# Moving softmax exponentials, a gate row and the last residual inside a TensorE-bound transformer block

## The chip, the cores and the metric

The kernel runs on one core of one Trainium2 chip. The metric is the device time of one launch in microseconds (us). Three plain runs of the kernel before took 769.52, 769.94 and 769.98 us; their median is 769.94 us. A separate execution was recorded by the profiler and took 769.86 us.

## The reference

The block has 2048 tokens of width D = 640. One conditioning vector `c` gives six rows of modulation. Attention is linear attention with a learned feature map (32 heads of 20 features), and the feed-forward part squares its ReLU. Everything is fp32.

```python
mod = (silu(c) @ w_mod).reshape(1, 6, 1, 640)
sa, ca, ga, sb, cb, gb = mod[:, 0], ..., mod[:, 5]
h = layernorm(x) * (1 + ca) + sa
q, k, v = heads(h @ wqkv)
pq = q @ w_phi;  pk = k @ w_phi                 # per head, 20 x 20
phi_q = concat(softmax(pq), softmax(-pq));  phi_k likewise
o = phi_q (phi_k^T v) / (phi_q (phi_k^T 1) + 1e-6)
x = x + ga * (o @ wo)
h = layernorm(x) * (1 + cb) + sb
r = relu(h @ w1 + b1) ** 2                      # 640 -> 1728
x = x + gb * (r @ w2 + b2)
```

## The kernel before

Tokens are worked on in 16 tiles of 128, mostly as 8 pairs (`NB` = 8, index `j`). A product of two fp32 matrices is made of three matmuls on a high and a low part of each operand; the high part is a ScalarE copy that rounds, and the low part a VectorE subtraction (`lo`, line 88). The program has three stages.

**Projections.** For every tile, k, v and (for tiles 0 to 11) q are projected, and phi_k^T v and its row sums are accumulated. The exponentials of q for tiles 0 to 11 (`KEPT` = 12) are computed here and parked in DRAM. The products of `c` with the sixth part of `w_mod`, which give the gate `gb`, are summed by VectorE in `gb_mac`, and TensorE turns them (`mod_turn`) into `mt5`, of which `mod_sum(5, gate_b)` makes a [128, 5] column tile. A gate is needed as a row that is the same on all 128 partitions: `spread_row` writes the columns element by element to a DRAM tile `GD` and reads that tile back with a broadcast. `biases` loads `b2` as such a row, before into a tile `b2s`.

**Attention output.** From about 255 to 389 us the loop over `j` runs with the order of TensorE, VectorE, ScalarE and GpSimd written out by hand. Per tile, `e_prod`, `e_recip` and `e_scale` (VectorE, and small steps on GpSimd) form the denominators and scale the q features. Per pair, `tr_e(j, gs)` turns the scaled features on TensorE in six groups (`te` in the profile) and ScalarE copies each group out (`ept`); `num` multiplies by phi_k^T v; `num_hi` (ScalarE) and `num_lo` (VectorE) split the result into `ot`; `do_wo` multiplies by `wo` (`pwo`). In iteration `j`, TensorE works on the output product of pair `j` and on `tr_e` and `num` of pair `j + 1`. The six `ept` copies of a pair share five buffers (tag `s4`), so the sixth copy waits until `num` has read the first. Tiles 12 to 15 still lack their exponentials: `q_chain(t, False)` makes the differences (`spread`, VectorE, tile `eq`), `exps` applies two exponentials of 128x640 on ScalarE, and `q_sums` reduces them on VectorE. `SPREAD` and `SUMS` say at which `j` tiles 13 and 14 get these steps. Each `do_wo` ends in ScalarE copies (`at`); `p_hi`, `p_lo` and `p_load` split and load the feed-forward weights in between.

**Feed-forward.** The loop over `j` (pairs) and `n` (7 pairs of feature blocks) runs `up` (matmul, ScalarE ReLU with bias, VectorE square), `split_a` and the `down` of the step before. From `PLAIN` = 2 on, most `down` steps use a Strassen-like scheme of seven products, with accumulators in PSUM banks `acc` (named "1" to "7" and "x"). "3" and "x" are the two halves of one bank, `acc3x`; "6" and "7" share the bank with tag `p67`. The results of a pair are combined (`first_combos`, `end`), multiplied by the gate row `gb_b` (`by_gate`) and added to the residual `XR`, to which the gated bias `bb` was added before (`add_bias`). For the last pair the final three blocks are plain products, which `last_downs` ends: quarter by quarter ("3", "x", "2", "4") it does the last products, and VectorE reads each finished quarter with `by_gate`, adds it to `Y` and stores it.

Of the kernel before, what the change touches and what calls it, by code (L numbers as in the profile page):

```python
# [8 lines left out]
F32 = mybir.dt.float32  # L9
# [42 lines left out]
def kernel(  # L52
# [64 lines left out]
    def row(tag, name):  # L117
        return (pc if tag in ("s3", "s4") else mem).tile([P, D], F32, tag=tag, name=name, bufs=BUFS[tag])
# [384 lines left out]
            nc.gpsimd.dma_start(w[2 * n : m, 0], w[2 * n : m, 1])  # L503

    ga_b = row("s4", "ga_b")
    b2s = []

    def biases():
        b2s.append(row("s1", "b2s"))
        nc.sync.dma_start(b2s[0], bass.AP(tensor=b2.tensor, offset=b2.offset, ap=[[0, P], [1, D]]))  # L510

    GB = []

# [19 lines left out]
    }  # L533
    gate_a = const.tile([P, NC], F32, name="gate_a")
    gate_b = const.tile([P, NC], F32, name="gate_b")
    LAST_COL = {7: (2, gate_a), 9: (3, cols_b[:, 0:5]), 11: (4, cols_b[:, 5:10])}
    SIDE = {
        2: lambda: mod_mac(2, 0, 1, 2),
# [590 lines left out]
    e_scale(3)  # L1129
    load_e(6)  # L1130
    e_prod(4)
    SPREAD, SUMS = {1: 1, 3: 2}, {2: 1, 4: 2}
    ln0 = None
    for j in range(NB):
        nxt = j + 1 < NB
        b, c = 2 * j + 5, 2 * j + 6
        te_at = (0, 1) if 0 < j < 6 else (1, 2)
        if j == 4:
            load_x1(0)
        if j < 5:  # L1140
            p_load()
        if j != 5:
            e_prod(b)
        e_recip(b - 1)
        e_scale(b - 1)
        if j == 5:
            q_chain(KEPT + 3, False)
            add_x(0, 0, 1)
            nc.vector.tensor_tensor(bb, b2s[0], gb_b, op=ALU.mult)
            ln0 = ln_parts(XM[0], "b0")  # L1150
        load_e(b + 2)
        def te(at):
            for i, gs in enumerate((range(3), (5, 3, 4))):
                if nxt and te_at[i] == at:
                    tr_e(j + 1, gs)

        do_wo(j, 0, 0)
        te(0)
        if j == 5:
            exps(EQ[KEPT + 3])  # L1160
            q_sums(KEPT + 3)
            e_prod(b)
        do_wo(j, 0, 1)
        if j == 7:
            t2(0, 0)
            t2(0, 1)
        te(1)
        if j == 5 or j == 6:
            next(ln0)
        if j in SUMS:  # L1170
            q_sums(KEPT + SUMS[j])
        e_prod(c)
        if j != 5:
            e_recip(b)
            e_scale(b)
        do_wo(j, 1, 0)
        if j == 7:
            t2(0, 2)
            t2(0, 3)
        te(2)  # L1180
        if nxt:
            num(j + 1)
            num_hi(j + 1)
        do_wo(j, 1, 1, 0, 8)
        if j == 7:
            t2(0, 4)
        if not nxt:
            do_wo(j, 1, 1, 8, 16)
        if nxt:
            do_wo(j, 1, 1, 8, 11)  # L1190
            num_lo(j + 1)
            do_wo(j, 1, 1, 11, 16)
        if j == 5:
            e_recip(b)
            e_scale(b)
        if j in SPREAD:
            q_chain(KEPT + SPREAD[j], False)
            exps(EQ[KEPT + SPREAD[j]])
        if j == 3:
            mod_sum(5, gate_b)  # L1200
            spread_row(1, gate_b, gb_b)
        load_e(c + 2)
        if j == 5:
            next(ln0)
        if 1 <= j < 6:
            p_hi()
        if j == 5:
            p_lo(4)
            p_load(4)
        if j == 6:  # L1210
            p_hi(4)
            p_lo(5)
            p_load(3)
        if j == 7:
            p_load(2)
# [148 lines left out]

    def acc(j, reg):

        bank_ = {"3": "3x", "x": "3x", "6": "67", "7": "67"}.get(reg, reg)
        if (j, bank_) not in ACC:
            if len(bank_) == 2:
                ACC[j, bank_] = psC.tile([P, 512], F32, tag=f"p{bank_}", name=f"acc{bank_}_{j}")  # L1370
            else:
                ACC[j, bank_] = psA.tile([P, 512], F32, tag="pj", name=f"acc{bank_}_{j}", bufs=4)
        t = ACC[j, bank_]
        return (j, bank_), t[:, :384] if len(bank_) == 1 else t[:, 256:] if reg in "x7" else t[:, :256]
# [39 lines left out]
    def add(o, a, b):  # L1414
        nc.vector.tensor_tensor(o, a, b, op=ALU.add)
# [115 lines left out]
    for j in range(NB):  # L1531
        if j <= PLAIN:
            if j:
                by_hand.__exit__(None, None, None)
            by_hand = tc.manual_schedule(engines={ET_.PE, ET_.DVE, ET_.Activation, ET_.Pool} | ({ET_.SP} if j != 1 else set()))
            by_hand.__enter__()
        for n in range(NP):
            down = lambda k: prev and (down_plain if plain(*prev) else down_pair)(*prev, k)
            twice = not plain(j, n)
            m = NP * j + n - NP - 1  # L1540
            if (j, n) == (NB - 1, NP - 1):
                for k in range(2):
                    up(j, 2 * n + k)
                    split_a(j, n, (k,))
                for i in range(2):
                    add(Y[j][i], Y[j][i], XR[j, i])
                break
            done = j - 1 if j and prev else None
            up(j, 2 * n)
            if prev and not plain(*prev):  # L1550
                split_s(*prev)
            down(0)
            if j < PLAIN:
                layer(j + 1, 2 * n, None if j else 0)
            if 0 < m < NP - 2:
                t_split(m - 1)
            if m == -1:
                t_load(0)
            if (j, n) == (PLAIN, 0):
                t_fetch(4)  # L1560
            if j >= PLAIN:
                if n == 5 + (j == PLAIN):
                    for i in range(2):
                        add_bias(j, i)
                layer(j + 1, 2 * n)
            prep(next(PREPS, 0))
            if j == 0:
                layer(j + 1, 2 * n, 1)
            if n == 0 and j:
                if j - 1 >= PLAIN:  # L1570
                    first_combos(j - 1)
                else:
                    Y[j - 1] = [row("s2", f"y{j - 1}_{i}") for i in range(2)]
                for r, i, c in (("3", 0, R), ("2", 0, L)):
                    end(j - 1, r, i, c)
            if n == 1 and j:
                gate(j - 1, 0)
                if j != PLAIN:
                    finish(j - 1, j < PLAIN)
            if n == 1 and j == PLAIN:  # L1580
                finish(j - 1, 0)
            if n == 2 and j == PLAIN:
                t_sums(NP - 2)
            if n == (2 if j > PLAIN else 1) and j:
                gate(j - 1, 1)
            if n == (5, 5, 5, 3)[min(j, 3)]:
                residual(j)
            for i in range(2):
                if n == 6 and j == 0:
                    add_bias(j, i)  # L1590
            if j == NB - 1 and n == 1:
                for k in range(NP - LAST, NP - 1):
                    plain_load(k)
            if j == NB - 1 and n == 3:
                for k in range(NP - LAST, NP - 1):
                    plain_split(k)
            if j == NB - 1 and n == NP - 2:
                for i in range(2):
                    by_gate(Y[j][i], Y[j][i], slice(0, D))
            up(j, 2 * n + 1)  # L1600
            if j >= PLAIN and n == 0:
                down(1)
            split_a(j, n)
            if twice:
                sums(j, n)
            if j < PLAIN or n:
                down(1)
            if m == NP + 1:
                t_split(NP - 2)
            ahead = (j, n) == (0, 3)  # L1610
            if ahead:
                layer(j + 1, 2 * n + 1)
            prep(next(PREPS, 0))
            if n == 0 and j:
                end(j - 1, "4", 1, L)
                end(j - 1, "x", 1, R)
            if n == (2 if j > PLAIN else 1 if j == PLAIN else 0) and j:
                finish(j - 1, j >= PLAIN)
            if not ahead:
                layer(j + 1, 2 * n + 1)  # L1620
            if 0 <= m < NP - 2:
                t_sums(m)
            if m == NP - 2:
                t_split(m - 1)
            if 0 < m + 1 < NP - 1:
                t_load(m + 1)
            if m == NP - 1:
                for i in range(2):
                    add_bias(j - 1, i)
            if j == NB - 1 and n == NP - LAST:  # L1630
                first_combos(j)
            prev = j, n
# [60 lines left out]
```

## Time and profile before

| | before |
|---|---|
| median of three runs | 769.94 us |
| profiled execution, time | 769.86 us |
| profiled execution, span first to last instruction | 768.2 us |
| TensorE matmul busy | 759.3 us (99%) |
| TensorE weight load busy | 739.8 us (96%) |
| VectorE busy | 593.8 us (77%) |
| ScalarE busy | 434.6 us (57%) |
| GpSimd busy | 144.2 us (19%) |
| granted TensorE clock | 1.000 |

The span is counted from the first to the last instruction; the execution's time has 1.66 us more around it. In the profile's names PE is TensorE (PEld its weight loads), DVE is VectorE, ACT is ScalarE, POOL is GpSimd, SP is the engine that issues most DMAs (SPq in the lists). A row of the timeline gives start and duration in us, the engine, the line, the operation, output and inputs, how many were merged, and in brackets the idle time before the first of them and what ended it.

### The profile page before, as it was taken

The page shows a single profiled execution, that of the slowest core. Times are in us where ns is not written, and L with a number is a line of the kernel's source. Part 1 is how long each engine was busy: PE and PEld are TensorE (multiplying, and loading weights), DVE is VectorE, ACT ScalarE, POOL GpSimd, SP SyncE. Part 2 cuts the span into 40 slices and gives each one's busy share as a digit, 9 for nine tenths or more (in the row PEclk, how much of TensorE's full clock was granted, in tenths as well). Part 3 has the DMA queues.
Part 4 walks back from the last instruction along what each step waited for, and adds up shares of the span by engine and source line. Part 5 has one row for each costly group of instructions (what it writes and reads, how often), then busy time and mean ns, then how long its engine had stood idle before and what let it go on. Part 6 is the DMA issues. An engine that isn't in the chain of part 4 may idle for free.

```text
span 768.2 us, 15300 instructions
## 1 busy us (share of the span) xinstructions
PE 759.3 (99%) x5967; PEld 739.8 (96%) x5967; DVE 593.8 (77%) x1083; ACT 434.6 (57%) x971; POOL 144.2 (19%) x301
## 2 busy tenths in 40 slices
PE   9999999999999999999999999999999999999997
PEld 8999999999999989888999999999999999999996
DVE  6598897989999999999565667866767666675666
ACT  5766756767843454545776647465553636445331
POOL 3001101101100255442101000231321313222110
PEclk9999999999999999999999999999999999999999
DMA  9811431343333344155356367996766758766450
GB/s 327 305 65 73 137 103 54 104 139 114 119 104 109 117 142 170 70 80 160 107 180 222 110 226 253 286 323 195 226 181 197 232 177 262 221 184 192 130 165 35
DMA packets 52151, 126.69 MB, mean 165 GB/s; under 512 B 7335, under 2 KB 8103, under 8 KB 52079
## 3 DMA queue, kind: packets, MB, share of 16 engines
q1 hardware_dynamic: 34744, 84.65, 33.1%
q0 software_dynamic: 14752, 35.76, 16.7%
q10 hardware_dynamic: 2583, 5.30, 1.8%
q8 instruction: 47, 0.77, 0.4%
q14 instruction: 25, 0.20, 0.1%
HBM read 95.70 MB, written 29.89 MB: 163 GB/s over the span
## 4 chain that ended last, share of the span: by engine, by line
PE 85%; DVE 8%; issue 2%; DMA 2%; POOL 2%; ACT 1%; SPq 0%; POOLq 0%; DVEq 0%
PE up L78 23%; PE acc L78 17%; PE pk L78 9%; PE pv L78 9%; PE pq L78 8%; PE pwo L78 5%; PE acc3x L78 5%; PE kvp L450 3%; DVE dn L879 2%; DVE scr L877 2%; DVE ezb L901 1%; PE tb L357 1%; PE te L921 1%; DMA ring_b<-td_b 1%; PE ta L357 1%
## 5 line engine op out<-in xcount | busy, mean ns | idle before, releaser
L78 PE MATMUL up<-h,w 128*128 128x256 f32 x1640 | 206.4, 278 | 0.0
L78 PEld LDWEIGHTS up<-h,w 128*128 128x128 f32 x1640 | 196.1, 188 | 0.0
L1250 ACT ACTIVATE ft<-up,b_t 128x256 f32<-128x256 f32 x104 | 48.9, 470 | 115.1 <-PE up L78 114.6
L78 PE MATMUL acc<-w,ra 128*128 128x384 f32 x452 | 97.4, 335 | 0.0
L1251 DVE TENSOR_TENSOR ft<-ft 128x256 f32<-128x256 f32 x104 | 44.1, 424 | 51.2 <-ACT ft L1250 49.6
L78 PE MATMUL pwo<-wo,ot 128*128 128x256 f32 (+3 forms) x512 | 80.8, 312 | 0.6 <-DVE ot L88 0.6
L78 PEld LDWEIGHTS pwo<-wo,ot 128*128 128x128 f32 (+1 forms) x512 | 74.5, 188 | 3.8 <-issue 2.7
L78 PE MATMUL pq<-wq,hT 128*128 128x384 f32 (+1 forms) x480 | 75.2, 312 | 0.0
L78 PEld LDWEIGHTS acc<-w,ra 128*128 128x128 f32 x452 | 72.7, 188 | 0.7 <-DVE ra L88 0.5
L78 PE MATMUL pk<-wk,hT 128*128 128x384 f32 (+1 forms) x480 | 72.7, 308 | 0.0
L78 PE MATMUL pv<-wv,hT 128*128 128x384 f32 (+1 forms) x480 | 71.7, 307 | 0.0
L78 PEld LDWEIGHTS pq<-wq,hT 128*128 128x128 f32 x480 | 71.1, 188 | 0.6 <-issue 0.2
L78 PEld LDWEIGHTS pk<-wk,hT 128*128 128x128 f32 x480 | 70.5, 188 | 0.4 <-issue 0.2
L78 PEld LDWEIGHTS pv<-wv,hT 128*128 128x128 f32 x480 | 70.1, 188 | 0.0
L88 DVE TENSOR_TENSOR ra<-ft,ra 128x384 fp32r<-128x384 f32 (+2 forms) x86 | 36.8, 448 | 32.9 <-ACT ra L1274 20.2
L78 PE MATMUL acc3x<-w,ra 128*128 128x256 f32 x248 | 42.3, 278 | 1.4 <-DVE end L1418 1.4
L1360 POOL DMA_DIRECT2D ring_a<-td_a x34 | 18.3, 537 | 125.5 <-PE acc L78 103.2
L1274 ACT ACTIVATE ra<-ft 128x384 fp32r<-128x384 f32 x48 | 25.2, 526 | 28.4 <-DVE ft L1251 22.4
L78 PEld LDWEIGHTS acc3x<-w,ra 128*128 128x128 f32 x248 | 39.5, 188 | 1.8 <-DVE end L1418 1.6
L1265 DVE TENSOR_TENSOR ft<-ft 128x128 f32<-128x128 f32 x136 | 33.3, 286 | 1.2
L441 DVE TENSOR_REDUCE sk<-ek 128x64 f32<-128x1280 f32 x16 | 23.7, 1484 | 12.4 <-ACT ek L436 10.8
L885 POOL TENSOR_TENSOR dn<-dn,rs_q 128x32 f32<-128x32 f32 x32 | 20.1, 629 | 68.1 <-DVE dn L879 67.8
(264 smaller groups left out, 1406.5 us busy)
## 6 DMA issues: line engine op xcount, KB each, us to landing
ring_c<-td_c POOLq DMA_DIRECT2D x34, 384.0 KB, 4.0
ring_a<-td_a POOLq DMA_DIRECT2D x34, 384.0 KB, 4.1
ring_b<-td_b POOLq DMA_DIRECT2D x34, 256.0 KB, 4.0
esp<-eq SPq DMA_DIRECT2D x12, 640.0 KB, 3.2
el<-esp SPq DMA_DIRECT2D x12, 640.0 KB, 4.0
rw<-in_w SPq DMA_DIRECT2D x23, 320.0 KB, 3.1
wm<-in_w_mod SPq DMA_DIRECT2D x20, 320.0 KB, 3.7
xb<-in_x SPq DMA_DIRECT2D x8, 640.0 KB, 4.0
```

Source lines behind the costliest of these rows:

```text
L78: nc.tensor.matmul(o, a, b, start=first and i == 0, stop=last and i == len(terms) - 1, skip_group_check=skip,)
L88: (eng or nc.vector).tensor_tensor(out_lo, full, hi.bitcast(F32), op=ALU.subtract)
L357: nc.tensor.transpose(p[:, i * P : (i + 1) * P], xn[:, i, d * P : (d + 1) * P], ident)
L441: nc.vector.tensor_reduce(s, heads(flat(e)), axis=AX.X, op=ALU.add)
L450: nc.tensor.matmul(kvp[g // 4][64 * c : 64 * c + 64, a : a + 2 * n].rearrange("p (s n) -> p s n", s=2), v[:, u], e[:, :, o : o + n], start ...
L877: nc.vector.tensor_tensor(z, flat(ET[t]), flat(zb), op=ALU.mult)
L885: nc.gpsimd.tensor_tensor(dn[:, s], dn[:, s], rs[:, 1 - s], op=ALU.mult)
L1250: nc.scalar.activation(r, p, AF.Relu, bias=b1_t[:, f : f + 1])
L1251: nc.vector.tensor_tensor(r, r, r, op=ALU.mult)
L1265: nc.vector.tensor_tensor(t[:, o], t[:, a], t[:, b], op=op)
L1274: nc.scalar.activation(a[:, 0, :3], t[:, :3], AF.Copy)
L1360: nc.gpsimd.dma_start(RING[j, n, r], TD[n][r].bitcast(F32R))
```

## The change

It has two parts, which touch different stages.

In the attention output, tile 13's exponentials leave the end of iteration 1 for the middle of iteration 2, behind the second group of `tr_e`, and its `q_sums` goes from iteration 2 to iteration 3; tile 14 stays as it was. The second three groups of `tr_e` run as 3, 4, 5 rather than 5, 3, 4 in iterations 1 to 5. `mod_sum(5, gate_b)` goes from the end of iteration 3 to the start of iteration 6. The gate row is no longer written column by column: in iteration 7 TensorE turns `gate_b` into [5, 128], ScalarE copies that to a new tile `gate_r`, and one DMA writes its five rows of 512 bytes to `GD`, which the broadcast then reads. `b2` is loaded straight into `bb`, and the product with the gate row leaves iteration 5 of the attention for the end of step (0, 4) of the feed-forward.

In the feed-forward's last pair, "x" gets a bank of its own, with the tag `p67` that "6" and "7" have left by then. `add_bias` of that pair comes at n = 4 instead of 5, and the two additions of the residual to `Y` come at n = 5, right behind `by_gate`, instead of at the end of n = 6.

```diff
     def biases():
-        b2s.append(row("s1", "b2s"))
-        nc.sync.dma_start(b2s[0], bass.AP(tensor=b2.tensor, offset=b2.offset, ap=[[0, P], [1, D]]))
+        nc.sync.dma_start(bb, bass.AP(tensor=b2.tensor, offset=b2.offset, ap=[[0, P], [1, D]]))
...
+    gate_r = pc.tile([NC, P], F32, name="gate_r")
...
-    SPREAD, SUMS = {1: 1, 3: 2}, {2: 1, 4: 2}
+    SPREAD, SUMS = {1: 1, 3: 2}, {3: 1, 4: 2}
...
+        if j == 6:
+            mod_sum(5, gate_b)
         if j == 5:
             q_chain(KEPT + 3, False)
             add_x(0, 0, 1)
-            nc.vector.tensor_tensor(bb, b2s[0], gb_b, op=ALU.mult)
...
-            for i, gs in enumerate((range(3), (5, 3, 4))):
+            for i, gs in enumerate((range(3), (3, 4, 5) if te_at[0] == 0 else (5, 3, 4))):
...
         if j == 5 or j == 6:
             next(ln0)
+        if j == 2:
+            exps(EQ[KEPT + 1])
         if j in SUMS:
             q_sums(KEPT + SUMS[j])
...
         if j == 7:
             t2(0, 4)
+            p = tp("gbt")[:NC, :P]
+            nc.tensor.transpose(p, gate_b, ident)
+            nc.scalar.activation(gate_r, p, AF.Copy)
+            nc.sync.dma_start(GD[1], gate_r)
+            nc.sync.dma_start(gb_b, GD[1].rearrange("c p -> (c p)")[None, :].to_broadcast([P, D]))
...
         if j in SPREAD:
             q_chain(KEPT + SPREAD[j], False)
-            exps(EQ[KEPT + SPREAD[j]])
-        if j == 3:
-            mod_sum(5, gate_b)
-            spread_row(1, gate_b, gb_b)
+            if j > 1:
+                exps(EQ[KEPT + SPREAD[j]])
...
     def acc(j, reg):
 
+        if (j, reg) == (NB - 1, "x"):
+            if (j, reg) not in ACC:
+                ACC[j, reg] = psC.tile([P, 512], F32, tag="p67", name="accx")
+            return (j, reg), ACC[j, reg][:, :256]
...
                     split_a(j, n, (k,))
-                for i in range(2):
-                    add(Y[j][i], Y[j][i], XR[j, i])
                 break
...
-                if n == 5 + (j == PLAIN):
+                if n == 5 + (j == PLAIN) - (j == NB - 1):
                     for i in range(2):
                         add_bias(j, i)
...
                     by_gate(Y[j][i], Y[j][i], slice(0, D))
+                    add(Y[j][i], Y[j][i], XR[j, i])
...
+            if (j, n) == (0, 4):
+                nc.vector.tensor_tensor(bb, bb, gb_b, op=ALU.mult)
```

More of the change, by code (lines that the diff above doesn't have):

```diff
@@ L505 @@
     ga_b = row("s4", "ga_b")
-    b2s = []
     def biases():
-        b2s.append(row("s1", "b2s"))
-        nc.sync.dma_start(b2s[0], bass.AP(tensor=b2.tensor, offset=b2.offset, ap=[[0, P], [1, D]]))
+        nc.sync.dma_start(bb, bass.AP(tensor=b2.tensor, offset=b2.offset, ap=[[0, P], [1, D]]))
     GB = []
```

## The prediction, made before the changed kernel ran

> **What bounds the kernel now.** I read the page first, then TensorE's own waits, then the timeline of each engine where those waits lie.
>
> ```profile
> span 768.2 us, 15300 instructions
> PE 759.3 (99%) x5967; PEld 739.8 (96%) x5967; DVE 593.8 (77%) x1083; ACT 434.6 (57%) x971; POOL 144.2 (19%) x301
> ...
> PE 85%; DVE 8%; issue 2%; DMA 2%; POOL 2%; ACT 1%; SPq 0%; POOLq 0%; DVEq 0%
> ```
>
> TensorE is busy for 759.3 of 768.2 us, so an edit can only win by closing one of its gaps, and it loses whatever it opens. The chain that ended last still runs through VectorE for 8% of the span, so there are stretches where VectorE sets the pace. The list of waits of PE and PEld names the gaps:
>
> ```profile
> PE acc3x L78 <- DVE end L1418: 1.4, 1, 1.4
> PE acc L78 <- DMA ring_b<-td_b: 0.7, 1, 0.7
> ...
> PE te L921 <- ACT ept L923: 0.3, 1, 0.3
> ...
> PEld acc3x L78 <- DVE end L1418: 1.6, 1, 1.6
> ```
>
> The first is at the very end (the bank that "3" and "x" share), the third is in the attention loop, and with it another of 0.57 us that the timeline below shows at 349.55. The change touches these; the second, a DMA wait in the feed-forward, I take as unchanged.
>
> A list of idle time misses matmuls that only run thinner. So I measure the attention loop by its period, the time from one `num` to the next on TensorE:
>
> ```profile
> 298.66 1.08 PE L78 MATMUL numa<-ept,kvd 120*64 120x256 f32 x8
> ...
> 314.15 1.08 PE L78 MATMUL numa<-ept,kvd 120*64 120x256 f32 x8
> 328.99 1.08 PE L78 MATMUL numa<-ept,kvd 120*64 120x256 f32 x8
> 343.78 1.08 PE L78 MATMUL numa<-ept,kvd 120*64 120x256 f32 x8
> 349.55 2.71 PE L78 MATMUL pwo<-wo,ot 128*128 128x384 f32 x14 [0.57 <-DVE ot L88]
> 359.33 1.08 PE L78 MATMUL numa<-ept,kvd 120*64 120x256 f32 x8
> 373.91 1.08 PE L78 MATMUL numa<-ept,kvd 120*64 120x256 f32 x8
> ```
>
> The last period, 373.91 - 359.33 = 14.58 us, has no wait in it. The four before are 15.49 (j = 2), 14.84, 14.79 and 15.55 (j = 5), so they lose 0.91 + 0.26 + 0.21 + 0.97 = 2.35 us together. That is the most the attention part of the change can win.
>
> **The exponentials of tile 13.** The loss at j = 2 is ScalarE's:
>
> ```profile
> 306.91 0.74 ACT L436 ACTIVATE eq<-eq 128x640 f32<-128x640 f32 x1 [2.99 <-DVE eq L433]
> ...
> 309.18 1.56 ACT L923 ACTIVATE ept<-te 120x512 f32<-120x512 f32 x3
> ...
> 314.85 0.60 ACT L923 ACTIVATE ept<-te 120x512 f32<-120x512 f32 x1 [2.57 <-PE numa L78]
> ...
> 315.71 0.60 ACT L950 ACTIVATE ot<-numa 128x512 fp32r<-128x512 f32 x1
> ```
>
> ScalarE stood 2.99 us at the head of its queue for VectorE's differences, and the `ept` copies queued behind it, without which TensorE has no free bank for the second group of `te`, began only at 309.18. After the change nothing stands there, and the 0.91 us at j = 2 goes. In the new place the exponentials stand behind the sixth `ept` copy, which itself waits for `num`. They take two times about 0.74 us, and push `num_hi` (315.71) back by up to 1.5 us, while TensorE's earlier `num` pulls it forward by 0.9: it comes at about 316.3. What waits for it is `num_lo`, on VectorE:
>
> ```profile
> 311.96 1.47 DVE L478 TENSOR_REDUCE rs_q<-eq 128x64 f32<-128x1280 f32 x1
> ...
> 318.52 0.68 DVE L88 TENSOR_TENSOR ot<-numa,ot 128x512 fp32r<-128x512 f32 x1
> ...
> 331.19 0.69 DVE L88 TENSOR_TENSOR ot<-numa,ot 128x512 fp32r<-128x512 f32 x1 [0.42 <-ACT ot L950]
> ...
> 336.37 0.81 DVE L310 TENSOR_REDUCE gate_b<-mt 128x5 f32<-128x640 f32 x1
> ...
> 348.82 0.68 DVE L88 TENSOR_TENSOR ot<-numa,ot 128x512 fp32r<-128x512 f32 x1
> ...
> 357.50 0.82 DVE L1149 TENSOR_TENSOR bb<-b2s,gb_b 128x640 f32<-128x640 f32 x1
> ```
>
> `num_lo` of pair 3 began at 318.52 because VectorE was full until then. With `q_sums` of tile 13 (311.96, 1.47 us) out of iteration 2 VectorE arrives at 317.05. The result of `num_hi`, 316.3 + 0.60 = 316.9, is there by then, so the moved exponentials cost TensorE nothing, with about 0.15 us to spare on the first piece; TensorE's need for this low part is what costs the 0.26 at j = 3, and it goes too.
>
> **What VectorE allows.** TensorE would then be 1.2 us ahead, but VectorE must follow. `q_sums` comes back in iteration 3, so the 1.47 us is only lent. VectorE truly saves two things up to the wait at 349.55: its idle 0.42 us at 331.19, which was a wait for ScalarE behind TensorE and goes when TensorE is earlier, and `mod_sum` (0.81 us at 336.37). So `num_lo` of pair 5 moves from 348.82 to about 347.6, and TensorE, which waits for it at 349.55, goes on 1.2 us earlier. That is the term I take: **-1.2 us**. Its bounds are -0.8 (`mod_sum` alone, if TensorE is not early enough to spare VectorE the idle 0.42) and -2.35 (all losses of the periods). After 349.55 VectorE gains another 0.82 from `bb`; the periods after it have no loss, so this wins nothing, it only keeps VectorE ahead. `mod_sum` at j = 6 falls into 5.75 us in which VectorE waits, and `bb` at (0, 4) into a wait of 1.69:
>
> ```profile
> 375.79 0.69 DVE L88 TENSOR_TENSOR ot<-numa,ot 128x512 fp32r<-128x512 f32 x1 [5.75 <-ACT ot L950]
> ...
> 416.80 0.83 DVE L88 TENSOR_TENSOR w<-rw,w 128x640 fp32r<-128x640 f32 x1 [1.69 <-ACT w L1014]
> ```
>
> Without these covers each would cost its 0.8 us. The order 3, 4, 5 of `te` makes the copy that waits for `num` the small one; I count it at nothing; at worst it costs a whole copy, the 0.60 us at 314.85, and a gain from it is within the 2.35 already.
>
> **The gate row.** TensorE gets one transpose more. Twelve took 1.47 us (end of the pipeline included), so one is **+0.1 us**:
>
> ```profile
> 321.81 1.47 PE L921 MATMUL te<-ident,ezb 128*120 128x128 f32 x12
> ```
>
> ScalarE's copy of [5, 128] comes behind the last `h` copy, where TensorE already has its operands; I take nothing, and at most the same 0.60 us of a far larger copy. On SP the write of the row and its broadcast read move from 337 us to about 390, in front of or among the loads of feed-forward weights. That is the one place where the change adds risk:
>
> ```profile
> gate<-gate_b SPq DMA_DIRECT2D x1, 2.5 KB, 11.5
> ...
> td_a<-tst_a SPq DMA_DIRECT2D x5, 384.0 KB, 2.3
> ...
> rw<-in_w SPq DMA_DIRECT2D x23, 320.0 KB, 3.1
> ...
> 392.90 0.33 SPq L1004 DMA_DIRECT2D rw<-in_w  x1
> ...
> 396.45 1.36 ACT L1014 ACTIVATE w<-rw 128x640 fp32r<-128x640 f32 x2
> ```
>
> The element-wise write took 11.5 us and the broadcast behind it held SP that long. A write to DRAM in whole rows took 2.3 us at 384 KB, so 2.5 KB in five rows should take no longer: issued at about 390.2 it lands at 392.5, and the weight load that stood until 392.90 is hardly touched. I take 0. The other end of the range is priced as a rival below. The Trainium skill, in "DMA: Bandwidth & Descriptors", section "Anatomy of one DMA — SWDGE (gpsimd) path", gives a DMA about 2.0 us that do not depend on its size; by that figure too this term would be 0, while by the row of 11.5 us it would be several us, so that figure fits the 2.3 us row and not the element-wise one.
>
> **The tail.** The last steps in order of time:
>
> ```profile
> 758.00 1.00 PE L78 MATMUL acc3x<-w,ra 128*128 128x256 f32 x5
> ...
> 758.48 1.56 DVE L1415 TENSOR_TENSOR y<-y,xr 128x640 f32<-128x640 f32 x2
> 759.96 0.42 DVE L1418 TENSOR_TENSOR end<-acc3x,gb_b 128x256 f32<-128x256 f32 x1
> ...
> 760.43 0.84 PE L78 MATMUL acc3x<-w,ra 128*128 128x256 f32 x5 [1.43 <-DVE end L1418]
> ```
>
> "3" is finished at 759.0. VectorE is still adding the residual to `Y`, reads "3" only at 759.96, and "x", in the same bank, may start after that read. With its own bank "x" follows "3" at once, and everything behind it moves: **-1.5 us**, between 1.43 (PE) and 1.63 (PEld, above). VectorE is no new bound, since the additions that kept it are gone and "3" can be read at 759.0. They go to n = 5, where they take the 1.55 us that `add_bias` leaves there, and `add_bias` goes into 1.99 us of waiting at n = 4:
>
> ```profile
> 745.09 0.43 DVE L1251 TENSOR_TENSOR ft<-ft 128x256 f32<-128x256 f32 x1 [1.99 <-ACT ft L1250]
> 746.79 1.83 DVE L1415 TENSOR_TENSOR y<-y,acc 128x256 f32<-128x256 f32 x4
> 748.88 1.55 DVE L1415 TENSOR_TENSOR xr<-xr,bb 128x640 f32<-128x640 f32 x2
> ...
> 751.56 0.51 PE L78 MATMUL acc3x<-w,ra 128*128 128x256 f32 x3
> ```
>
> The new bank is the one "6" and "7" leave when `first_combos` has read them, at 746.79 + 1.83 = 748.6; "x" first needs it at 751.56, 2.9 us later. No wait is added.
>
> **The sum.** -1.2 + 0.1 - 1.5 = -2.6 us. The profiled execution took 769.86 us, 0.08 below the median of 769.94, so the forecast is 769.86 - 2.6 = 767.3 us. With the bounds: -2.35 + 0.1 - 1.63 gives 766.0, and -0.8 + 0.6 + 0.6 + 0.1 - 1.43 gives 768.9.
>
> **Rivals.**
>
> 1. *The attention part gives back what it wins, and the tail alone is left.* For it: VectorE has 0.15 us to spare at 317 us, the exponentials of tile 14 stay in the old place, and `q_sums` in iteration 3 could push `num_lo` of pair 4. Against it: `mod_sum` leaves a stretch where VectorE waits for nothing. Time: 769.86 - 1.5 + 0.1 = 768.5.
> 2. *The tail wait only changes its name:* "x" or "2" meets another reader, or VectorE becomes the last in line. Against it are the 2.9 us above. Then only the attention part counts: 769.86 - 1.2 + 0.1 = 768.8.
> 3. *Slower: SP is held at 390 us.* If the turned row's write also takes 11.5 us, it lands at 401.7 instead of 392.5; the load of 392.90 is issued at 402.0 and lands at 405.1. ScalarE wants it for the second of the two copies at 396.45, so at about 397.1, and stands 8 us. Behind it are the copies that TensorE's next `down` needs; allowing some 1 us of slack there TensorE stops for 7 us, and with the other terms it is 769.86 - 2.6 + 7 = 774.3. It decides from a write of about 3.5 us on (397.1 - 3.1 - 0.3 - 390.2). For it: the only row of such a write is 11.5 us. Against: that one moved 640 single elements.
> 4. *The change doesn't do what it says,* because SP's order, which isn't written out in this stage, or the moved buffers of weights undo it: 769.9.
>
> **How the numbers follow.** A measurement of this kernel can tell about 0.2%, 1.54 us, from no change, so faster means below 768.4. The forecast, with both parts, has 0.71; only the far end of its range, where all bounds meet, lies above that, so 0.69 of it count as faster and 0.02 as same. Rival 1 has 0.13; its 768.5 lies at the edge, so 0.05 of it count as faster and 0.08 as same. Rival 2 has 0.06 (same), rival 3 0.06 (slower), rival 4 0.04 (same). Faster 0.69 + 0.05 = 0.74, same 0.02 + 0.08 + 0.06 + 0.04 = 0.20, slower 0.06. The range of 8 in 10 is that of the forecast's bounds, in which rivals 1 and 2 lie: 766.0 to 768.9.
>
> **What would show it.** In the profile after: no PE wait on `end` in the tail, and `acc` of "2" starting about 1 us after "3" ends; the period at j = 2 near 14.6 us with no 2.99 us stand on ScalarE before the exponentials; a small rest of the wait on `ot` at j = 5, since VectorE still paces that stretch; the write of `gate` near 390 us landing in 2 to 3 us. Wrong would be: periods at j = 2 to 5 that sum to no less than before; an ACT wait on a weight DMA at 395 to 402 us; a PE wait on `accx`.

## The result, and the profile after

The changed kernel took 766.31 us (median of five runs, 766.05 to 766.75), and the kernel before, run beside it, 769.93 us. The ratio is 0.9956, with a 95% interval of 0.9945 to 0.9967, so it is faster by 3.6 us, where 2.6 had been forecast. The profiled execution took 766.05 us, with a span of 764.3 instead of 768.2 us.

From the page of the changed kernel, below it TensorE's own waits in full, and last the one wait on `ot` in the list of its weight loads:

```profile
span 764.3 us, 15303 instructions
PE 758.5 (99%) x5968; PEld 739.7 (97%) x5968; DVE 593.9 (78%) x1083; ACT 435.6 (57%) x972; POOL 144.9 (19%) x301
...
PE 91%; DVE 7%; DMA 1%; issue 0%; SPq 0%; ACT 0%; DVEq 0%
...
PE warm L625 <- POOL bdc L155: 1.1, 1, 1.1
PE foldk L280 <- DVE bd_t L248: 0.2, 1, 0.2
PE foldk L280 <- DMA raw_k<-in_wk: 0.2, 1, 0.2
...
PEld pwo L78 <- DVE ot L88: 0.4, 1, 0.4
```

All four waits that the list of before had behind the first 20 us are gone, the one on `ring_b` among them, which the change doesn't touch. The timeline of TensorE in the attention loop:

```profile
283.12 1.08 PE L78 MATMUL numa<-ept,kvd 120*64 120x256 f32 x8
298.55 1.08 PE L78 MATMUL numa<-ept,kvd 120*64 120x256 f32 x8
313.18 1.08 PE L78 MATMUL numa<-ept,kvd 120*64 120x256 f32 x8
327.84 1.08 PE L78 MATMUL numa<-ept,kvd 120*64 120x256 f32 x8
342.88 1.08 PE L78 MATMUL numa<-ept,kvd 120*64 120x256 f32 x8
357.91 1.08 PE L78 MATMUL numa<-ept,kvd 120*64 120x256 f32 x8
372.52 1.08 PE L78 MATMUL numa<-ept,kvd 120*64 120x256 f32 x8
...
387.70 4.49 PE L78 MATMUL up<-h,w 128*128 128x256 f32 x38
```

The periods at j = 2 to 5 are 14.63, 14.66, 15.04 and 15.03 us; against 14.58 they lose 1.04 instead of 2.35 us. The gain is 1.31 us, and the feed-forward's first matmul comes 1.30 us earlier (389.00 to 387.70). ScalarE and VectorE around it:

```profile
314.16 0.72 ACT L436 ACTIVATE eq<-eq 128x640 f32<-128x640 f32 x1
...
315.78 0.59 ACT L949 ACTIVATE ot<-numa 128x512 fp32r<-128x512 f32 x1
...
317.11 0.68 DVE L88 TENSOR_TENSOR ot<-numa,ot 128x512 fp32r<-128x512 f32 x1
...
335.82 0.74 ACT L436 ACTIVATE eq<-eq 128x640 f32<-128x640 f32 x1 [2.73 <-DVE eq L433]
...
347.43 0.68 DVE L88 TENSOR_TENSOR ot<-numa,ot 128x512 fp32r<-128x512 f32 x1
```

Tile 13's exponentials no longer wait for anything (314.16 has no idle before it), and `num_lo` of pair 3 starts at 317.11 instead of 318.52. Tile 14's still stand, now 2.73 us (2.23 before), and that is where the loss at j = 4 shows. The gate row on SP, and the tail:

```profile
388.65 0.28 SPq L1192 DMA_DIRECT2D gate<-gate_r  x1
389.84 0.33 SPq L1193 DMA_DIRECT2D gb_b<-gate  x1
391.61 0.33 SPq L1003 DMA_DIRECT2D rw<-in_w  x1
...
755.89 1.00 PE L78 MATMUL acc3x<-w,ra 128*128 128x256 f32 x5
...
756.72 0.73 PE L78 MATMUL accx<-w,ra 128*128 128x256 f32 x5
756.92 0.43 DVE L1427 TENSOR_TENSOR end<-acc3x,gb_b 128x256 f32<-128x256 f32 x1 [0.59 <-PE acc3x L78]
757.29 2.94 PE L78 MATMUL acc<-w,ra 128*128 128x384 f32 x16
```

The broadcast read, which waits for the row's write, follows 1.19 us after that write was issued, and the weight load behind it goes out at 391.61, 1.29 us earlier than before, as everything there does. In the tail "x" starts 0.83 us after "3" (before: 2.43).

### The profile page after: what moved, and what is told of

Read it like the earlier page. It is cut to its first block, busy times and chain, and to the rows that moved or that the text cites. A ratio compares the mean times of both kernels' runs of the same rounds, so it can differ in the third digit from the quotient of the medians.

```text
span 764.3 us, 15303 instructions
## 1 busy us (share of the span) xinstructions
PE 758.5 (99%) x5968; PEld 739.7 (97%) x5968; DVE 593.9 (78%) x1083; ACT 435.6 (57%) x972; POOL 144.9 (19%) x301
## 4 chain that ended last, share of the span: by engine, by line
PE 91%; DVE 7%; DMA 1%; issue 0%; SPq 0%; ACT 0%; DVEq 0%
PE up L78 24%; PE acc L78 18%; PE pq L78 9%; PE pk L78 9%; PE pv L78 9%; PE pwo L78 6%; PE acc3x L78 5%; PE kvp L450 3%; PE te L920 1%; DVE dn L878 1%; DVE scr L876 1%; DVE ezb L900 1%; PE tb L357 1%; PE ta L357 1%; DVE ot L88 1%; PE foldq L280 1%
## 5 line engine op out<-in xcount | busy, mean ns | idle before, releaser
L78 PE MATMUL acc3x<-w,ra 128*128 128x256 f32 x231 | 39.8, 278 | 0.0
L78 PEld LDWEIGHTS acc3x<-w,ra 128*128 128x128 f32 x231 | 37.2, 188 | 0.2 <-DVE ra L88 0.2
```

Of the source, the lines that this page charges most:

```text
L78: nc.tensor.matmul(o, a, b, start=first and i == 0, stop=last and i == len(terms) - 1, skip_group_check=skip,)
```

## The experiments

The first theory (A in the expectations) was: VectorE paces the loop; the attention part is worth 1.2 to 1.3 us, half through ScalarE's order and half through VectorE's work; the tail is worth 1.7; the wait on `ring_b` came and went by chance. This table splits the trace of every kernel that ran into three stretches, in us. The loop runs from the second `numa` to the feed-forward's first `up`; the feed-forward from there to the last five matmuls of "3"; the tail from there to the end of the span. The wait on `ring_b` is the PE wait inside the feed-forward. Each row is one trace. The loop is 105.78 to 105.91 us in the five kernels that leave it as it was, and 104.51 to 104.58 in the three with the attention part of the change (attn_only, after, after_again).

| kernel | loop | feed-forward | of it, ring_b wait | tail | ratio to before (95%) |
|---|---|---|---|---|---|
| before | 105.82 | 369.00 | 0.68 | 10.20 | 1 |
| before_again | 105.78 | 367.94 | 0 | 10.19 | 1.0002 (0.9993 to 1.0011) |
| te_only | 105.79 | 369.66 | 1.40 | 10.15 | 1.0003 (0.9994 to 1.0012) |
| exps_only | 105.17 | 368.96 | 0.72 | 10.20 | 0.9994 (0.9984 to 1.0004) |
| gate_only | 105.18 | 369.72 | 1.42 | 10.22 | 0.9993 (0.9982 to 1.0003) |
| attn_only | 104.52 | 368.17 | 0 | 10.15 | 0.9980 (0.9971 to 0.9990) |
| tail_only | 105.90 | 368.40 | 0.18 | 8.47 | 0.9977 (0.9968 to 0.9987) |
| bank_only | 105.91 | 368.26 | 0 | 8.66 | 0.9974 (0.9965 to 0.9983) |
| adds_only | 105.78 | 368.37 | 0 | 9.31 | 0.9986 (0.9977 to 0.9994) |
| after | 104.58 | 368.19 | 0 | 8.41 | 0.9956 (0.9945 to 0.9967) |
| after_again | 104.51 | 367.93 | 0 | 8.48 | 0.9958 (0.9945 to 0.9970) |
| both_later | 103.99 | 368.79 | 0.48 | 8.49 | 0.9960 (0.9946 to 0.9974) |
| both_later_2 | 104.02 | 369.09 | 0.83 | 8.51 | 0.9958 (0.9945 to 0.9970) |
| columns_late | 104.46 | 378.85 | 0.58 | 8.51 | 1.0099 (1.0085 to 1.0114) |

**The two parts alone.** attn_only is the diff without its three pieces in `acc`, `add_bias` and the residual; tail_only is those three pieces alone.

> The attention part alone, with the tail of before. Theory A (VectorE paces the loop, the two parts add up, and the missing wait on ring_b is chance): the periods j = 2 to 5 lose 1.1 us in all instead of 2.35, TensorE enters the feed-forward 1.3 us earlier, the tail keeps its wait of 1.4 us on end, and the time is 769.9 - 1.2 = 768.7, or 767.9 if the ring_b wait of 0.7 us happens to be absent. Rival B (the attention part moves the feed-forward against its DMAs and so removes the ring_b wait): the ring_b wait is gone here, and 767.9.

> The own bank for x and the sooner bias and residual alone, on the attention of before. Theory A: no wait on end, last products 1.7 us earlier, 769.9 - 1.7 = 768.2, or 767.4 if the ring_b wait happens to be absent. Rival B: the ring_b wait of 0.7 us is there, as in before, since nothing ahead of it has moved, and 768.2.

attn_only took 767.83 us beside 769.12 of before, tail_only 767.56. The loop alone gives 1.3 us, the tail alone 1.7, and each leaves the other's stretch as it was; the product of the two ratios, 0.9957, is the ratio of the whole change. tail_only tells the two theories on `ring_b` apart only weakly: ahead of the feed-forward its program is that of before, and it shows 0.18 us, neither 0.7 nor 0.

**The attention part in pieces.**

```diff
exps_only:
-    SPREAD, SUMS = {1: 1, 3: 2}, {2: 1, 4: 2}
+    SPREAD, SUMS = {1: 1, 3: 2}, {3: 1, 4: 2}
+        if j == 2:
+            exps(EQ[KEPT + 1])
-            exps(EQ[KEPT + SPREAD[j]])
+            if j > 1:
+                exps(EQ[KEPT + SPREAD[j]])
gate_only:
+        if j == 6:
+            mod_sum(5, gate_b)
-        if j == 3:
-            mod_sum(5, gate_b)
-            spread_row(1, gate_b, gb_b)
...            (and the turned row, bb loaded directly and multiplied at (0, 4))
te_only:
-            for i, gs in enumerate((range(3), (5, 3, 4))):
+            for i, gs in enumerate((range(3), (3, 4, 5) if te_at[0] == 0 else (5, 3, 4))):
```

> Only tile 13's exponentials and row sums moved; mod_sum, the column-wise gate write, bb and the te order as before. Theory A: the period at j = 2 falls from 15.49 to 14.65 and that at j = 3 to about 14.65, but VectorE saves only its 0.42 us of idling (and some 0.2 between the pieces of num_lo), so the wait on ot at j = 5 grows from 0.57 to about 1.1 and the feed-forward starts 0.5 to 0.6 us earlier: 769.4. Rival C (ScalarE alone was the limit): the loss stays away, the feed-forward starts 1.1 us earlier: 768.8.

> Only the gate row's path: mod_sum to iteration 6, the turned row, bb at (0, 4). Exponentials, te order and tail as before. Theory A: VectorE saves mod_sum's 0.8 us ahead of the wait at j = 5, so that wait goes almost wholly and the feed-forward starts 0.6 to 0.7 us earlier, the transpose of 0.1 us counted: 769.2. Rival C: the gate path was hidden, nothing moves: 769.9 to 770.0. The row's write lands within 2.5 us and no ScalarE copy waits for a weight load, by both.

> Only the order 3, 4, 5 of the second te groups, on the kernel before. Theory A: worth nothing, every period within 0.1 us of before's, ratio 1.000. Rival G (the smaller last copy lets num_hi and so num_lo come earlier): VectorE's idle 0.42 us at j = 3 shrinks to about 0.2 and the feed-forward starts 0.2 us earlier.

TensorE's timeline, exps_only first and then gate_only:

```profile
282.77 1.08 PE L78 MATMUL numa<-ept,kvd 120*64 120x256 f32 x8
...
298.24 1.08 PE L78 MATMUL numa<-ept,kvd 120*64 120x256 f32 x8
...
312.94 1.08 PE L78 MATMUL numa<-ept,kvd 120*64 120x256 f32 x8
...
327.63 1.08 PE L78 MATMUL numa<-ept,kvd 120*64 120x256 f32 x8
...
342.76 1.08 PE L78 MATMUL numa<-ept,kvd 120*64 120x256 f32 x8
...
348.51 2.70 PE L78 MATMUL pwo<-wo,ot 128*128 128x384 f32 x14 [0.55 <-DVE ot L88]
...
387.94 4.26 PE L78 MATMUL up<-h,w 128*128 128x256 f32 x36
```

```profile
282.88 1.08 PE L78 MATMUL numa<-ept,kvd 120*64 120x256 f32 x8
...
388.06 4.15 PE L78 MATMUL up<-h,w 128*128 128x256 f32 x35
```

Each shortens the loop by 0.65 us, and together they give the 1.3 us of attn_only: theory C, in either form, is out. In exps_only the periods at j = 2 and 3 fall to 14.70 and 14.69, a gain of 0.94, and a part is given back: j = 4 grows from 14.79 to 15.13, behind tile 14's exponentials. The wait on `ot` did not grow to 1.1 us as I expected; it stayed at 0.55 us, so I had the place of the loss wrong there and its size about right. In gate_only that wait is gone (j = 5: 14.76), as expected. The medians of these two (768.78 and 768.70 beside 769.12) can't be told from that of before, since both intervals include 1; the 0.65 us rest on the traces. te_only changes the split of the periods (15.36, 15.04, 14.66 and 15.62) by up to 0.2 us, twice what I expected, but not the loop: on the kernel before, the order of the groups is worth nothing.

**The tail in pieces.** bank_only is the hunk in `acc`, adds_only the three hunks of `add_bias` and `add`.

> Only x in its own bank; bias and residual of the last pair where they were. Theory A: x follows 3 at once, TensorE ends 1.5 us earlier, but VectorE still adds the residual first and then has four by_gate and add pairs to do, so the last store comes only about 1.2 us earlier: 768.7 (less 0.7 if the ring_b wait is absent). Rival D (the bank does all of it): 1.7 us, 768.2.

> Only the sooner bias and residual; 3 and x share a bank. Theory A: VectorE reads 3 as soon as it is finished, so the wait on end shrinks from 1.43 to about 0.5 to 0.7 us but stays: 0.9 us earlier, 769.0 (less 0.7 if the ring_b wait is absent). Rival D: the wait stays at 1.4 and the time at 769.9.

VectorE at the end of bank_only, and then TensorE's wait in adds_only:

```profile
757.32 1.56 DVE L1419 TENSOR_TENSOR y<-y,xr 128x640 f32<-128x640 f32 x2
758.79 0.42 DVE L1422 TENSOR_TENSOR end<-acc3x,gb_b 128x256 f32<-128x256 f32 x1
...
761.44 0.55 DVE L1422 TENSOR_TENSOR end<-acc,gb_b 128x384 f32<-128x384 f32 x1
```

```profile
759.12 0.86 PE L78 MATMUL acc3x<-w,ra 128*128 128x256 f32 x5 [0.52 <-DVE end L1418]
```

The bank alone makes the tail 8.66 us, 1.54 less than before; the sooner additions alone 9.31, 0.89 less. The two overlap: together 8.41 to 8.51. With the bank alone TensorE no longer waits, but VectorE runs without a gap to the end (no idle is marked at 758.79 or 761.44) and is last by 0.2 us. With the additions alone the wait shrinks from 1.43 to 0.52 us, since 3's reading still keeps "x" out of the bank. Theory D is out for the additions, and for the bank it is nearly right.

**The wait on ring_b.**

> The kernel before, unchanged, profiled once more. Theory A (the wait on ring_b is chance): the periods repeat within 0.15 us (15.5, 14.8, 14.8, 15.5), the wait on end is 1.4 us again, but the ring_b wait may be anything from 0 to 1.4 us, and the time from the feed-forward's first matmul to the tail is 368.2 us plus that wait. Rival B (the wait belongs to the code): 0.7 us again. Ratio 1.000.

The fetch of `ring_b` that is issued at 508.15 us in the first profile of before and at 508.12 in the second, its matmuls, and the range of landing times from 507 us on (two fetches); first profile, second profile, and te_only:

```profile
515.61 0.62 PE L78 MATMUL acc<-ring_b,rs 128*128 128x256 f32 x3 [0.68 <-DMA ring_b<-td_b]
DMA to landing us min/median/max: 4.8/6.1/7.4
```

```profile
514.73 0.50 PE L78 MATMUL acc<-ring_b,rs 128*128 128x256 f32 x3
DMA to landing us min/median/max: 4.4/5.3/6.3
```

```profile
516.34 0.62 PE L78 MATMUL acc<-ring_b,rs 128*128 128x256 f32 x3 [1.40 <-DMA ring_b<-td_b]
DMA to landing us min/median/max: 4.8/6.5/8.1
```

TensorE needs the tile 6.6 us after the fetch was issued (514.73 - 508.12). It lands after 6.3 to 8.1 us, and the wait is what lies over about 6.6. The same kernel shows 0.68 us and none. Over the 14 traces the wait is 0 to 1.42 us, and the rest of the feed-forward, columns_late aside, is 367.9 to 368.4 us in all of them. So the wait in the first profile of before and its absence in that of after need no cause in the change, and can be chance; whether its average differs between the two kernels stays open. This fetch landed after 6.3 to 8.1 us in the six kernels with the old order of exponentials and gate, and after 5.7 to 7.6 us in five with the attention part (all but columns_late); these ranges overlap too much to settle it.

**The price of the slow write.** columns_late is the changed kernel with this in iteration 7 in place of the turned row, and no `mod_sum` in iteration 6:

```diff
+            mod_sum(5, gate_b)
+            spread_row(1, gate_b, gb_b)
```

> The changed kernel, but mod_sum in iteration 7 and the gate written column by column as before, at the place of the turned row, so that the slow write meets the weight loads. Theory A (rival 3 of the prediction, priced): the write takes about 11 us, SP is held from 389 to about 400, ScalarE's weight copies stand about 8 us, TensorE about 7: 766.3 + 7 = 773. Rival E (the loads have more slack than the rows show, or the write is faster here): 766.3 to 767.5.

SP, ScalarE, TensorE, and TensorE's granted clock (the column of 0.80, 0.50 and 0.68) in columns_late:

```profile
390.12 0.38 SPq L328 DMA_DIRECT2D gate<-gate_b  x1
...
400.57 0.33 SPq L329 DMA_DIRECT2D gb_b<-gate  x1
400.99 1.56 SPq L1003 DMA_DIRECT2D rw<-in_w  x1
...
402.24 0.74 ACT L1013 ACTIVATE w<-rw 128x640 fp32r<-128x640 f32 x1 [6.65 <-DMA rw<-in_w]
...
407.80 1.33 PE L78 MATMUL acc<-w,ra 128*128 128x384 f32 x3 [7.23 <-ACT ra L1274]
...
411.17 2.85 PE L78 MATMUL up<-h,w 128*128 128x256 f32 x15
...
415.57 1.86 PE L78 MATMUL up<-h,w 128*128 128x256 f32 x15
...
400.00:405.00 5.00, 0.57 (x6) 0.37 (x4) 0.83 (x1) 0.74 (x1) 0.00 (x0) 0.80 0.70 167
405.00:410.00 5.00, 2.20 (x8) 2.12 (x9) 3.29 (x7) 3.88 (x8) 0.00 (x0) 0.50 0.97 336
410.00:415.00 5.00, 5.00 (x29) 5.00 (x28) 1.69 (x3) 0.73 (x2) 0.00 (x0) 0.68 1.00 349
```

It took 776.97 us, not 773. The chain is the one that was priced: the write holds SP for 10.4 us, the weight copies wait for their load, TensorE stops for 7.23 us. On top comes a cost that I had not counted: behind the stop the clock is granted at half, and fifteen `up` matmuls take 2.85 us instead of 1.86. From 407.80 to the `up` at 415.57 TensorE needs 7.77 us; for the same matmuls the changed kernel needs 5.14 (400.07 to 405.21), so the slower clock costs 2.6 us. The feed-forward is 378.85 - 368.2 = 10.6 us longer: 7.4 of standing from start to start (7.23 by the row), 0.6 of `ring_b`, and 2.6 of the slower clock. So the column-wise write could not have moved to this place as it was. Whether the turned row was needed at all is not shown: no run writes the columns right behind `mod_sum` in iteration 6. In the changed kernel `mod_sum` ends there at 369.1, and SP issues nothing from 369.5 to 381.3, a gap of 11.8 us, where such a write took 9.7 to 11.5.

**What is left in the loop.** The losses of the changed kernel at j = 4 and j = 5 seem, by the trace, to have two causes, tile 14's exponentials and `num_lo` of pair 5 behind `e_scale`. both_later turns both orders, ran twice, the second time beside the changed kernel:

```diff
-        if j != 5:
+        if j not in (4, 5):
             e_recip(b)
             e_scale(b)
...
         te(0)
+        if j == 4:
+            exps(EQ[KEPT + 2])
...
-        if j == 5:
+        if j in (4, 5):
             e_recip(b)
             e_scale(b)
...
-            if j > 1:
-                exps(EQ[KEPT + SPREAD[j]])
```

> The changed kernel, and in iteration 4 tile 13's e_recip and e_scale behind num_lo of pair 5, and tile 14's exponentials behind the first group of te. Theory A (what is left is VectorE's order at j = 5 and ScalarE's stand at j = 4): the periods at j = 4 and 5 fall from 15.04 and 15.03 to about 14.65, 0.8 us less: 765.5. Rival F (VectorE's amount of work is the limit, not its order): the loss only moves to te of pair 6 or 7, 766.3.

> The same kernel as both_later, now on the same chip as the changed one. Theory A: its attention loop is 0.6 us shorter again (periods at j = 4 and 5 of 14.6 and 14.9), so its median is 0.6 us below after_again's; the ring_b wait by chance moves single runs by as much. Rival F: no lower than after_again's.

> The changed kernel, unchanged, profiled once more and beside both_later_2. Theory A: the periods repeat (14.6, 14.7, 15.0, 15.0), no wait on end, a ring_b wait from 0 to 1.4 us by chance, 0.9955 to 0.9965 of before. Rival B: no ring_b wait again.

TensorE's timeline of both_later_2:

```profile
327.80 1.08 PE L78 MATMUL numa<-ept,kvd 120*64 120x256 f32 x8
342.43 1.08 PE L78 MATMUL numa<-ept,kvd 120*64 120x256 f32 x8
357.31 1.08 PE L78 MATMUL numa<-ept,kvd 120*64 120x256 f32 x8
...
387.10 5.17 PE L78 MATMUL up<-h,w 128*128 128x256 f32 x44
```

The periods at j = 4 and 5 fall to 14.63 and 14.88, and the loop is 0.5 us shorter in both traces. VectorE has the same work in both kernels, so it was VectorE's and ScalarE's order that left some 0.55 us of the 0.91 lost there. The two orders were turned together, so what each gave is not shown. The 0.30 us left at j = 5 lie in front of `num`: in both_later ScalarE stands 2.52 us for the differences of tile 15, and `num` at 356.97 waits for an `ept` copy that is queued behind its exponentials. In time it can't be seen: 766.38 us beside 766.33 of the changed kernel, each with a range of over 1 us, and the profiled runs had a `ring_b` wait of 0.83 and of 0. So both_later is not shown to be faster.

## Why the prediction was right

The direction was right and 766.31 us lies in the range of 766.0 to 768.9, but at its low end. Step by step:

- *The exponentials of tile 13.* The loss at j = 2 went from 0.91 to 0.05 us and that at j = 3 from 0.26 to 0.08. `num_hi` came at 315.78 (forecast 316.3), `num_lo` at 317.11 (317.05).
- *What VectorE allows.* `num_lo` of pair 5 moved to 347.43 (forecast 347.6), the loop shortened by 1.24 us with the transpose in it (forecast 1.1). gate_only and exps_only show both savings, each 0.65. That the sum fits is in part luck: the idle time was taken as 0.42 and gave 0.65, `mod_sum` as 0.8, of which the transpose takes 0.1 back. The small rest of the wait on `ot` that was foretold is the 0.4 us of the weight loads; in TensorE's own list it no longer appears. Not foreseen: j = 4 lost 0.46 instead of 0.21, since TensorE comes to j = 4 1.15 us earlier and tile 14's exponentials start only 0.67 us earlier (335.82 instead of 336.49).
- *The gate row.* The write took 1.2 us, less than the 2.3 of the nearest row and the 2 to 3 named as a sign; the feed-forward between its ends was untouched. The figure of about 2.0 us of the Trainium skill ("DMA: Bandwidth & Descriptors", "Anatomy of one DMA — SWDGE (gpsimd) path") is for another issuing path, and here 1.2 us was measured. `bb` ran at 421.9, not in the wait at 416.80 that I named, and cost nothing there either.
- *The tail* is the term that was mis-sized: 1.7 to 1.8 us instead of 1.5 (tail 10.20 to between 8.41 and 8.51), above its upper bound of 1.63. I took the idle time of the row, 1.43. But the row counts from the modelled end of "3", 759.0, and without the wait "x" does not start at that end: in the profile after it starts at 756.72, 0.17 us before the 756.89 at which "3" ends by its row. The loss is the distance from start to start, 2.43 - 0.83 = 1.60, and 0.1 more for "x" itself, whose five matmuls took 0.84 us from a standstill and 0.73 in flow. For the same reason "2" starts 0.4 us after the end of "3" by its row (757.29 and 756.89), not about 1 us.
- *The step that failed* is "a DMA wait in the feed-forward, I take as unchanged". It was 0.68 us in one profile and none in the other. The 3.9 us between the two spans are 1.24 in the loop (forecast 1.1), 1.79 in the tail (1.5), 0.06 ahead of the loop, and 0.81 in the feed-forward, where nothing was forecast. These 0.81 can't be credited to the change, since the unchanged kernel shows the wait and its absence; that they fell on this side is, as far as the runs tell, luck, and they are most of why the result lies at the low end. With profiles that both lack the wait (before_again, 767.1, and after_again, 764.1) the difference is 3.0 us: 1.3 from the loop and 1.7 from the tail. The medians' 3.6 us in the first comparison and 2.8 in the last lie on either side of it.

Of the rivals, 1, 2 and 4 were wrong, since each part kept its gain, and 3 did not come; columns_late shows that it was real, at 10.6 us rather than 7.

## What to carry to other kernels

Measure what a wait costs by the distance from start to start in a period that has none, not by the idle time of its row. Where an engine stands at the head of its queue for a slower one, as ScalarE did for 2.99 us here, moving that one instruction behind what the bound engine needs is worth its wait only as far as the engine that paces the stretch can follow; look for work to take off that engine in the same edit. And look at a second profile of the unchanged kernel before calling any wait on a DMA constant.

## What the hardware showed

A stop of 7.2 us on TensorE cost 2.6 us more in a lower clock behind it. In slices of half a microsecond columns_late is granted 1.00 up to 402.5 us, 0.50 from 403.0 to 413.0 and 1.00 again from 413.5, while TensorE stands from 400.6 to 407.8. So the clock fell 2.4 us after the last matmul and came back about 5.4 us after the first one behind the stop. The Trainium skill, "TensorE: Matmul & The Clock Gate", section "Part 1: The HAM clock gate (the "warmup" mystery)", says that the clock falls to half after an idle window of about 3.4 us and returns after as long a busy one. The trace agrees on the half and on the return, but here 2.4 us without a matmul were enough for the fall. And 640 single elements took 10.4 us to reach DRAM where the same 2.5 KB in five rows took 1.2.
